# Attention and two MoE layers on one core: the product of pp and w_in as float32 products of one head each

## The chip, the cores and the metric

One core of one Trainium2 chip runs the whole program. The metric is device time in microseconds (us): the median of three runs of the kernel before is 1433.44 us (1433.17 to 1434.22).

## The reference, cut to what matters

```python
p_packed = sm_attn(p, k, v)              # 32 packed rows per head: softmax(p k^T / 8) v
out = sm_attn(q, p_packed, p_packed)     # batch 8, heads 8, 576 tokens, head size 64
x = out.transpose(0, 2, 1, 3).reshape(4608, 512)
h = x @ w_in                             # w_in is 512 x 2048
g = s * np.maximum(h, 0.0) ** 2 + b
x2 = g @ w_out                           # w_out is 2048 x 512
a, b2 = x2 @ w1, x2 @ w2                 # second layer, 1024 wide
return ((a * b2) @ w3) @ w_out2
```

The kernel does not form `x`. With A the softmax of the second attention (tokens by 8 heads x 32 packed rows, 256 wide) and pp the packed result of the first, x @ w_in is A @ W' with W' = pp @ w_in, where each head's 32 rows of pp meet the 64 rows of w_in that belong to that head. W' is 256 x 2048 for each batch. This case is about how W' is made.

## The kernel before, in words

**Stages.** From 0 to about 90 us the first attention of batches 0 to 3 runs (units u of four heads, N1 = 8 units), w_in is decoded from the 64-bit input, and W' of batches 0 and 1 is made (`W_pair`, L524). From 92 to about 840 us a loop over 256 steps (L1011) does the first MoE layer: a batch has 32 steps (two halves of 288 tokens, 16 blocks of 128 columns of d_ff). A step has six products into `hps` (A by W') and twelve into `xps` (g by w_out), each a `mm3`: three float32r products of high and low parts in place of one float32 product. Between those steps stand the rest: the second attention of later batches (`qtp` L186 transposes, `scp` L200, `atp` L234), the first attention of batches 4 to 7 (units 8 to 15, placed by `plan`, L911, into steps that have room: `ktp` L352, `s1p` L378, `etp` L444, `pvp` L466, `ppp` L480), the decoding of w1, w2, w3 and w_out2 (`job`), and W' of batches 2 to 7. After 840 us comes the second MoE layer, which this case does not touch.

**pp.** `ppT` holds pp transposed: 128 partitions are two heads of 64, and for each pair of heads and each batch 64 columns, the two heads' 32 packed rows side by side. Half of those 128 x 64 numbers are zeros, since a head's columns are zero in the other head's 64 partitions (L471 multiplies by `rec`, which has a zero for the other head). `D_ev` (L477) writes it from a transpose.

**W' of batches 0 and 1** (`W_pair`, eight calls in iterations 6 to 9 of the first loop): two tiles of w_in (two pairs of heads, 512 columns) and both batches, four float32 products of 128 rows by 64 columns, one to each half of two PSUM tiles. A float32 product is two matmul records in the trace. Evicted by ACT as the high part, DVE as the low part (batch 0), and ACT as a plain copy (batch 1), which is split later (`split_wp`).

**W' of batches 2 to 7** (three times 16 tiles of w_in, one per step from step 17 of an odd batch on, NW = 16): `W_load` (L860) brings a tile of the decoded w_in back from DRAM four steps ahead, `W_split` (L503) splits it on ACT and DVE one step ahead, and `W_tile` (L509) makes both batches' columns of one pair of heads in one `mm3` of 128 rows by 128 columns, N = 512, into one PSUM tile of the pair `a2`. `pp_split` (L489) splits pp first, once per pair of batches (steps 46, 110 and 172). The steps of `wsteps` (L906) have no room for `plan`.

**Order.** Each engine runs its instructions in the order that they were given when the program was built. A scheduler sets that order, from a timeline simulation of its own; only what `keep_in_program_order` names is tied down. PSUM tiles named `a2` are two buffers that everything beside `hps` and `xps` shares in the loop of 256 steps.

Of the kernel before, what the change touches and what calls it, by code (L numbers as in the profile page):

```python
# [22 lines left out]
def fused_kernel(  # L23
# [80 lines left out]
    ident = const.tile([P, P], F32, name="ident")  # L104
    odd = const.tile([P, 2, 1], F32, name="odd")
# [58 lines left out]
    if True:  # L164
# [322 lines left out]
        pps, sw, wst, wch = {}, {}, {}, {}  # L487

        def pp_split(bp):  # L489

            hi = stg.tile([P, NPAIR, P], F32R, tag="pph", name="pph", bufs=1)
            lo = stg.tile([P, NPAIR, P], F32R, tag="ppl", name="ppl", bufs=1)
            for o in range(2):
                for bb in range(2):
                    c = slice(64 * (bb ^ o), 64 * ((bb ^ o) + 1))
                    split(hi[:, o::2, c], lo[:, o::2, c], ppT[:, bp, o::2, bb, :], pin="hi")
            pps[bp] = (hi, lo)
# [5 lines left out]
        def W_split(k, src):  # L503
            hi = stg.tile([P, FC], F32R, tag="sh", name="sh", bufs=2)
            lo = stg.tile([P, FC], F32R, tag="sl", name="sl", bufs=2)
            split(hi, lo, src)
            sw[k] = (hi, lo)

        def W_tile(bp, k, ps):  # L509

            fc, pr = divmod(k, NPAIR)
            ph, pl = pps[bp]
            wh, wl = sw.pop(k)
            mm3(ps, ph[:, pr, :], pl[:, pr, :], wh, wl, True, True)
            if pr == 0:
# [3 lines left out]
            h0, h1 = (slice(64 * ((pr + bb) % 2), 64 * ((pr + bb) % 2 + 1)) for bb in range(2))  # L519
# [4 lines left out]
        def W_pair(j, ps):  # L524

            fc, c = divmod(j, 2)
            for pr in (2 * c, 2 * c + 1):
                for bb in range(2):
                    h = slice(64 * ((pr + bb) % 2), 64 * ((pr + bb) % 2 + 1))
                    ins = nc.tensor.matmul(  # L530
                        ps[bb][h], ppT[:, 0, pr, bb, :], win_at(fc * NPAIR + pr), start=True, stop=True
                    )
                    if bb:
                        tc.keep_in_program_order(ins)
            if c == 0:
                wch[0, fc] = wch_tiles()
                wst[1, fc] = wch_p.tile([P, 2, FC], F32, tag="wpst", name="wpst", bufs=4)
            hi, lo = wch[0, fc]
            split(hi[:, c], lo[:, c], ps[0])
            nc.scalar.copy(wst[1, fc][:, c], ps[1])  # L540
# [68 lines left out]
        make_identity(nc, ident)  # L609
        for h in range(4):  # L610
# [23 lines left out]
        def w_pair(j):  # L634
            wps = q_ps if j % 2 == 0 else kt_ps
            W_pair(j, [wps("wps") for _ in range(2)])
# [230 lines left out]
        WR = 17  # L867
# [37 lines left out]

        wsteps = {2 * FB1 * n_ + WR + w for n_ in range(1, B - 1, 2) for w in range(NW)}  # L906

# [67 lines left out]
        PPS = (46, 110, 172)  # L975
# [467 lines left out]
```

## Time and profile before

| | before |
|---|---|
| median of 3 runs | 1433.44 us |
| the profiled execution | 1435.98 us |
| its span, first to last instruction | 1434.2 us |
| granted TensorE clock, mean | 0.997 |
| busy: PE, DVE, ACT | 98%, 63%, 52% |

PE is the matmul engine (TensorE) and PEld its weight loads; DVE is VectorE and ACT is ScalarE. A record of PE has a duration that includes the way through the array, so records overlap. What a matmul costs the engine is the time from its start to the next one's start; the timeline view shows starts. Consecutive records of one kind are merged there into one row: its start, the time to the end of its last record, and how many.

### The profile page before, as it was taken

The page shows a single profiled execution, that of the slowest core. Times are in us where ns is not written, and L with a number is a line of the kernel's source. Part 1 is how long each engine was busy: PE and PEld are TensorE (multiplying, and loading weights), DVE is VectorE, ACT ScalarE, POOL GpSimd, SP SyncE. Part 2 cuts the span into 40 slices and gives each one's busy share as a digit, 9 for nine tenths or more (in the row PEclk, how much of TensorE's full clock was granted, in tenths as well). Part 3 has the DMA queues.
Part 4 walks back from the last instruction along what each step waited for, and adds up shares of the span by engine and source line. Part 5 has one row for each costly group of instructions (what it writes and reads, how often), then busy time and mean ns, then how long its engine had stood idle before and what let it go on. Part 6 is the DMA issues. An engine that isn't in the chain of part 4 may idle for free.

```text
span 1434.2 us, 28727 instructions
## 1 busy us (share of the span) xinstructions
PE 1410.8 (98%) x11233; PEld 1332.8 (93%) x11233; DVE 899.5 (63%) x1770; ACT 750.7 (52%) x1617; POOL 3.9 (0%) x38
## 2 busy tenths in 40 slices
PE   8999999999999999999999999999999999999997
PEld 6579999999999999998999988999999999999997
DVE  5786544656556666567878346476675756757556
ACT  4686555776566766557867534143332433324323
POOL 0000000000000000000000000000000000000000
PEclk9999999999999999999999999999999999999999
DMA  8975221232453543454655352775675857757551
GB/s 294 342 242 167 60 65 34 83 91 83 138 154 101 156 127 100 124 161 134 182 163 195 96 185 82 236 245 166 194 226 166 251 167 207 222 161 216 161 162 44
DMA packets 177574, 228.90 MB, mean 160 GB/s; under 512 B 55584, under 2 KB 109856, under 8 KB 177440
## 3 DMA queue, kind: packets, MB, share of 16 engines
q1 hardware_dynamic: 177440, 227.08, 52.4%
q8 instruction: 89, 1.46, 0.4%
q14 instruction: 45, 0.37, 0.1%
HBM read 182.98 MB, written 44.04 MB: 158 GB/s over the span
## 4 chain that ended last, share of the span: by engine, by line
PE 89%; DMA 3%; ACT 3%; DVE 3%; SPq 1%; issue 1%; ACTq 0%; DVEq 0%
PE xps L86 9%; PE xps L89 9%; PE xps L90 9%; PE prod L86 7%; PE prod L90 7%; PE prod L89 7%; PE hps L90 4%; PE hps L86 4%; PE hps L89 4%; PE yps L89 4%; PE yps L90 4%; PE yps L86 4%; PE scp L200 2%; DMA raw<-in_moe_w_in_dram 2%; PE qtp L186 1%; PE wps L530 1%
## 5 line engine op out<-in xcount | busy, mean ns | idle before, releaser
L89 PE MATMUL xps<-gl,wo 128*128 128x288 f32 (+1 forms) x1024 | 302.5, 298 | 1.2 <-DVE gl L757 1.2
L90 PE MATMUL xps<-gh,wo 128*128 128x288 f32 (+1 forms) x1024 | 301.3, 298 | 0.0
L86 PE MATMUL xps<-gh,wo 128*128 128x288 f32 (+1 forms) x1024 | 291.9, 299 | 0.8 <-ACT xst L783 0.8
L86 PE MATMUL prod<-xc,whl 128*128 128x384 f32 x672 | 226.2, 337 | 3.1 <-ACT Ta L1083 2.0
L90 PE MATMUL prod<-xc,whl 128*128 128x384 f32 x672 | 225.0, 335 | 0.0
L89 PE MATMUL prod<-xc,whl 128*128 128x384 f32 x672 | 224.8, 335 | 0.0
L89 PEld LDWEIGHTS xps<-gl,wo 128*128 128x128 f32 x1024 | 192.7, 188 | 4.9 <-issue 1.9
L90 PEld LDWEIGHTS xps<-gh,wo 128*128 128x128 f32 x1024 | 192.4, 188 | 2.8 <-issue 1.9
L86 PEld LDWEIGHTS xps<-gh,wo 128*128 128x128 f32 x1024 | 188.1, 188 | 3.8 <-ACT xst L783 1.0
L745 ACT ACTIVATE r<-hps 128x288 f32<-128x288 f32 x256 | 104.4, 409 | 118.9 <-PE hps L90 111.3
L757 DVE TENSOR_TENSOR gl<-r,gh 128x288 fp32r<-128x288 f32 x256 | 115.7, 454 | 80.6 <-ACT r L754 77.0
L1083 ACT COPY Ta<-prod 128x384 f32<-128x384 f32 x96 | 46.1, 480 | 215.4 <-PE prod L90 214.6
L86 PE MATMUL hps<-ATh,wpl 128*128 128x288 f32 x512 | 153.0, 299 | 1.4 <-ACT r L745 0.7
L90 PE MATMUL hps<-ATh,wph 128*128 128x288 f32 x512 | 152.7, 298 | 0.0
L89 PE MATMUL hps<-ATl,wph 128*128 128x288 f32 x512 | 152.4, 298 | 0.0
L89 PE MATMUL yps<-w4c,op 128*128 128x256 f32 x504 | 142.2, 282 | 0.0
L90 PE MATMUL yps<-w4c,op 128*128 128x256 f32 x504 | 142.1, 282 | 0.0
L86 PE MATMUL yps<-w4c,op 128*128 128x256 f32 x504 | 140.9, 280 | 0.0
L86 PEld LDWEIGHTS prod<-xc,whl 128*128 128x128 f32 x672 | 126.2, 188 | 7.6 <-ACT Ta L1083 4.1
L89 PEld LDWEIGHTS prod<-xc,whl 128*128 128x128 f32 x672 | 126.2, 188 | 0.0
L90 PEld LDWEIGHTS prod<-xc,whl 128*128 128x128 f32 x672 | 126.1, 188 | 0.0
L754 ACT ACTIVATE r<-r 128x288 f32<-128x288 f32 x256 | 112.8, 444 | 4.9
(167 smaller groups left out, 2519.5 us busy)
## 6 DMA issues: line engine op xcount, KB each, us to landing
whl<-whl SPq DMA_DIRECT2D x336, 256.0 KB, 3.1
raw<-in_moe_w_dram SPq DMA_DIRECT2D x32, 512.0 KB, 4.7
raw<-in_moe_w_out_dram SPq DMA_DIRECT2D x24, 512.0 KB, 5.1
x<-win SPq DMA_DIRECT2D x48, 256.0 KB, 2.8
q<-in_q_dram SPq DMA_DIRECT2D x72, 128.0 KB, 3.7
x<-xst SPq DMA_DIRECT2D x16, 576.0 KB, 3.8
out_dram<-O SPq DMA_DIRECT2D x72, 128.0 KB, 2.4
raw<-in_moe_w_in_dram SPq DMA_DIRECT2D x16, 512.0 KB, 7.1
```

Of the source, the lines that this page charges most:

```text
L86: ins = nc.tensor.matmul(ps, wl, xh, start=start, stop=False, **kw)
L89: nc.tensor.matmul(ps, wh, xl, start=False, stop=False, **kw)
L90: nc.tensor.matmul(ps, wh, xh, start=False, stop=stop, **kw)
L186: nc.tensor.transpose(ps[:, pr * P:pr * P + n], src[:n, 2 * pr:2 * pr + 2, :].rearrange("p h d -> p (h d)"), ident[:n, :n],)
L200: nc.tensor.matmul(ps[sl, c:c + 64], qT[b, t][:, pr, sl], ppT[:, b // 2, pr, b % 2, :], start=True, stop=True,)
L530: ins = nc.tensor.matmul(ps[bb][h], ppT[:, 0, pr, bb, :], win_at(fc * NPAIR + pr), start=True, stop=True)
L745: nc.scalar.activation(r, ps[:, :HS], AF.Relu)
L754: nc.scalar.activation(r, r, AF.Square)
L757: nc.vector.tensor_tensor(out=gl[:, :HS], in0=r, in1=gh[:, :HS].bitcast(F32), op=ALU.subtract)
L1083: tc.keep_in_program_order(nc.scalar.copy(out, src))
```

## The change

The array has, for products of 64 rows by 32 columns, eight places: two halves of the rows by four quarters of the columns. The change makes W' of all batches by `W_pair`, now with products of one head each: 64 rows of `ppT` by the 32 columns of one head, float32, N = 512. Two tiles of w_in (i), two batches (bb) and the two heads of a pair (r) make eight products, and the places are chosen so that the eight differ in place. That puts the two heads of the odd batch the other way round, so `ppT` of odd batches is written with its two groups of 32 columns exchanged: `D_ev` multiplies by a permutation `swap` in place of the transpose by `ident`. In the loop of 256 steps the 48 tiles of w_in become 24 pairs, at the steps WAT of odd batches, loaded at the steps WLD; `W_split`, `pp_split` and `W_tile` are gone, and a pair takes both `a2` buffers at once. The tags of some later tiles change with that (`wl` in place of `sh`, `sl`, `pph`).

```diff
@@ D_ev
-            nc.tensor.transpose(ps[:, :P], PVX.pop(u).rearrange("p o d -> p (o d)"), ident)
+            src = PVX.pop(u).rearrange("p o d -> p (o d)")
+            if b % 2:
+                nc.tensor.matmul(ps[:, :P], src, swap, start=True, stop=True)
+            else:
+                nc.tensor.transpose(ps[:, :P], src, ident)
...
-        def W_tile(bp, k, ps):
...
-            mm3(ps, ph[:, pr, :], pl[:, pr, :], wh, wl, True, True)
...
-            split(hi[h0, pr // 2], lo[h0, pr // 2], ps[h0])
-            d = wst[2 * bp + 1, fc][h1, pr // 2, :]
-            nc.scalar.copy(d, ps[h1])
...
+        def W_pair(bp, j, ps, src):
+
+            fc, c = divmod(j, 2)
+            for i in range(2):
+                for bb in range(2):
+                    for r in range(2):
+                        rows = slice(D * r, D * (r + 1))
+                        o = NP * (r ^ bb)
+                        h = 64 * (i ^ bb) + o
+                        ins = nc.tensor.matmul(
+                            ps[bb][h:h + NP], ppT[rows, bp, 2 * c + i, bb, o:o + NP], src[i][rows],
+                            start=True, stop=True,
+                        )
+                        if bp == 0 and bb:
+                            tc.keep_in_program_order(ins)
...
             split(hi[:, c], lo[:, c], ps[0])
-            nc.scalar.copy(wst[1, fc][:, c], ps[1])
+            nc.scalar.copy(wst[2 * bp + 1, fc][:, c], ps[1])
...
+        for o in range(2):
+            nc.gpsimd.tensor_copy(
+                swap.rearrange("p (a o n) -> p a o n", o=2, n=NP)[:, :, o],
+                ident.rearrange("p (a o n) -> p a o n", o=2, n=NP)[:, :, 1 - o],
+            )
...
-        def W_load(k):
-            wx[k] = dec.tile([P, FC], F32, tag="x", name="x", bufs=XB)
-            nc.sync.dma_start(out=wx[k], in_=win_d[k])
+        def W_load(j):
+            wx[j] = []
+            for k in (2 * j, 2 * j + 1):
+                wx[j].append(stg.tile([P, FC], F32, tag="wl", name="wl", bufs=6))
+                nc.sync.dma_start(out=wx[j][-1], in_=win_d[k])
...
-        WR = 17
+        WAT = (19, 20, 24, 25, 27, 28, 30, 31)
+        WLD = (13, 14, 16, 20, 21, 25, 26, 28)
...
-        wsteps = {2 * FB1 * n_ + WR + w for n_ in range(1, B - 1, 2) for w in range(NW)}
+        wsteps = {2 * FB1 * n_ + w for n_ in range(1, B - 1, 2) for w in WAT}
...
+            nn, k = divmod(idx, 2 * FB1)
+            if nn % 2 == 1 and nn + 1 < B:
+                for j in range(len(WAT)):
+                    if k == WLD[j]:
+                        W_load(j)
+                    if k == WAT[j]:
+                        W_pair((nn + 1) // 2, j, [a2_ps("wps") for _ in range(2)], wx.pop(j))
```

**The order on PE in the loop of 256 steps.** Before, around the first W' tiles of batches 2 and 3 (out<-in by the names of the program, then the size of the output; L86, L89 and L90 are the three products of a `mm3`):

```order
L89 MATMUL xps<-gl,wo_1932 128x288
L90 MATMUL xps<-gh,wo_1932 128x288
L86 MATMUL xps<-gh,wo_1932 128x288
L86 MATMUL wps<-sh,ppl 128x512
L89 MATMUL wps<-sl,pph 128x512
L90 MATMUL wps<-sh,pph 128x512
L89 MATMUL xps<-gl,wo_1932 128x288
L90 MATMUL xps<-gh,wo_1932 128x288
L86 MATMUL wps<-sh,ppl 128x512
L89 MATMUL wps<-sl,pph 128x512
L90 MATMUL wps<-sh,pph 128x512
L86 MATMUL hps<-ATh,wpl 128x288
```

And in the changed program, around the first two pairs of the same batches (L507 is the product of `W_pair` there):

```order
L90 MATMUL hps<-ATh,wph 128x288
L86 MATMUL xps<-gh,wo_1617 128x288
L89 MATMUL xps<-gl,wo_1617 128x288
L90 MATMUL xps<-gh,wo_1617 128x288
L507 MATMUL wps<-wl,ppT 32x512 x4
L86 MATMUL xps<-gh,wo_1617 128x288
L89 MATMUL xps<-gl,wo_1617 128x288
L90 MATMUL xps<-gh,wo_1617 128x288
L86 MATMUL xps<-gh,wo_1617 128x288
L89 MATMUL xps<-gl,wo_1617 128x288
L90 MATMUL xps<-gh,wo_1617 128x288
L507 MATMUL wps<-wl,ppT 32x512 x4
```

The three products of a tile stood together, 48 times. The eight of a pair stand as two runs of four, the first run into one PSUM tile (batch bb = 0) and the second into the other, with full-array products between them. Over the loop there are 44 such runs: 40 of four and 4 of eight. Four of the runs follow `scp` directly.

**The order on PE in the first stage.** Before, from the fifth pair on (winx is decoded w_in; `etp` and `wps` are 128 rows by 64 columns, `pvp` and `s1p` 64 by 32, `ppp` the full array):

```order
L460 MATMUL pvp<-v,E1T 32x64 x32
L530 MATMUL wps<-winx_150,ppT 64x512 x2
L430 MATMUL etp<-ident,E_1011 64x64 x10
L530 MATMUL wps<-winx_150,ppT 64x512 x2
L480 MATMUL ppp<-ident,pvx 128x128
L430 MATMUL etp<-ident,E_1011 64x64 x8
L530 MATMUL wps<-winx_151,ppT 64x512 x2
```

And in the changed program, where L461 is the line of `pvp` and L431 that of `etp`:

```order
L461 MATMUL pvp<-v,E1T 32x64 x36
L507 MATMUL wps<-winx_151,ppT 32x512 x4
L431 MATMUL etp<-ident,E_1022 64x64 x10
L507 MATMUL wps<-winx_151,ppT 32x512 x4
L485 MATMUL ppp<-ident,pvx 128x128
L431 MATMUL etp<-ident,E_1022 64x64 x8
L507 MATMUL wps<-winx_152,ppT 32x512 x4
```

Where two products stood, four of half the rows and half the columns stand. Over the first stage the 32 products before make 15 runs, one of four and the rest of two; the 64 after make 17 runs: three of eight, six of four, and eight of one to three.

## Rows read from the trace of the kernel before

**Rows 1.** The page: busy us of each engine, share, instructions; then the chain by engine.

```profile
PE 1410.8 (98%) x11233; PEld 1332.8 (93%) x11233; DVE 899.5 (63%) x1770; ACT 750.7 (52%) x1617; POOL 3.9 (0%) x38
...
PE 89%; DMA 3%; ACT 3%; DVE 3%; SPq 1%; issue 1%; ACTq 0%; DVEq 0%
```

**Rows 2.** Two stretches: length, busy us of PE, PEld, DVE, ACT, POOL, clock, DMA.

```profile
54.50:90.00 35.50, 34.57 (x571) 17.48 (x570) 28.04 (x66) 24.99 (x56) 0.57 (x8) 1.00 0.94 330
...
95.00:840.00 745.00, 740.82 (x6172) 707.68 (x6171) 460.98 (x1122) 495.51 (x1165) 2.68 (x24) 1.00 0.40 120
```

**Rows 3.** Timeline of PE, a W' tile in the loop: start us, us, instruction, count.

```profile
249.56 0.30 PE L90 MATMUL xps<-gh,wo 128*128 128x288 f32 x1
249.70 0.39 PE L86 MATMUL wps<-sh,ppl 128*128 128x512 f32 x1
...
250.40 0.29 PE L86 MATMUL xps<-gh,wo 128*128 128x288 f32 x1
```

**Rows 4.** Groups by form, 95 to 840 us: count, busy us, mean ns, idle before.

```profile
L81 DVE TENSOR_TENSOR wpl<-wps,wph 64x512 fp32r<-64x512 f32 x48 | 33.1, 689 | 24.1 <-ACT wph L78 23.0
...
L81 DVE TENSOR_TENSOR sl<-x,sh 128x512 fp32r<-128x512 f32 x48 | 32.8, 682 | 13.0 <-ACT sh L78 12.5
...
L78 ACT CAST sh<-x 128x512 fp32r<-128x512 f32 x48 | 29.7, 619 | 13.7 <-DMA x<-win 13.2
...
L78 ACT CAST wph<-wps 64x512 fp32r<-64x512 f32 x48 | 27.8, 580 | 16.4 <-PE wps L90 15.8
...
L522 ACT COPY wpst<-wps 64x512 f32<-64x512 f32 x48 | 27.8, 578 | 1.8 <-DVE wpl L81 1.0
...
L86 PE MATMUL wps<-sh,ppl 128*128 128x512 f32 x48 | 19.3, 403 | 0.8 <-ACT wpst L522 0.5 <-ACT qT L192 0.4
```

**Rows 5.** Timeline of PE around a late s1p: float32, 64 rows by 32 columns.

```profile
176.61 0.29 PE L86 MATMUL xps<-gh,wo 128*128 128x288 f32 x1
176.74 0.30 PE L89 MATMUL xps<-gl,wo 128*128 128x288 f32 x1
176.97 0.69 PE L378 MATMUL s1p<-kT,pTd 64*32 64x288 f32 x8
177.59 0.40 PE L90 MATMUL xps<-gh,wo 128*128 128x288 f32 x1
177.83 0.29 PE L86 MATMUL xps<-gh,wo 128*128 128x288 f32 x1
```

**Rows 6.** Timeline of PE in the first stage: W' pairs beside etp, s1p and pvp.

```profile
61.27 1.08 PE L530 MATMUL wps<-winx,ppT 128*64 128x512 f32 x4
62.27 0.62 PE L370 MATMUL s1p<-kT,pTd 64*32 64x256 f32 x2
...
81.83 0.97 PE L460 MATMUL pvp<-v,E1T 64*32 64x64 f32 x50
82.73 1.08 PE L530 MATMUL wps<-winx,ppT 128*64 128x512 f32 x4
83.64 0.75 PE L430 MATMUL etp<-ident,E 128*64 128x64 f32 x20
84.22 1.03 PE L530 MATMUL wps<-winx,ppT 128*64 128x512 f32 x4
85.18 0.33 PE L480 MATMUL ppp<-ident,pvx 128*128 128x128 f32 x1
```

**Rows 7.** The page's DMA issues: out<-in, count, KB each, median us to landing.

```profile
x<-win SPq DMA_DIRECT2D x48, 256.0 KB, 2.8
```

**Rows 8.** Timeline: the last ppp of the first stage, with its releaser.

```profile
89.76 0.33 PE L480 MATMUL ppp<-ident,pvx 128*128 128x128 f32 x1 [0.41 <-DVE pvx L471]
```

**Rows 9.** Timeline of PE around a late ppp, a transpose on the full array.

```profile
605.26 0.27 PE L480 MATMUL ppp<-ident,pvx 128*128 128x128 f32 x1
605.37 0.60 PE L186 MATMUL qtp<-ident,q 128*128 128x128 f32 x4
```

More of the change, by code (lines that the diff above doesn't have):

```diff
@@ L104, in fused_kernel @@
     ident = const.tile([P, P], F32, name="ident")
+    swap = const.tile([P, P], F32, name="swap")
     odd = const.tile([P, 2, 1], F32, name="odd")
@@ L484, in D_ev @@
             )
[L487 to L497, printed above, removed]
+        wst, wch = {}, {}
         def wch_tiles():
@@ L501, in wch_tiles @@
                     wch_p.tile([P, 2, FC], F32R, tag="wpl", name="wpl", bufs=4))
[L503 to L507, printed above, removed]
-        def W_tile(bp, k, ps):
-            fc, pr = divmod(k, NPAIR)
-            ph, pl = pps[bp]
-            wh, wl = sw.pop(k)
-            mm3(ps, ph[:, pr, :], pl[:, pr, :], wh, wl, True, True)
-            if pr == 0:
+        def W_pair(bp, j, ps, src):
[12 more added lines that the diff above has]
+                            tc.keep_in_program_order(ins)
+            if c == 0:
                 wch[2 * bp, fc] = wch_tiles()
@@ L518, in W_tile @@
             hi, lo = wch[2 * bp, fc]
-            h0, h1 = (slice(64 * ((pr + bb) % 2), 64 * ((pr + bb) % 2 + 1)) for bb in range(2))
-            split(hi[h0, pr // 2], lo[h0, pr // 2], ps[h0])
-            d = wst[2 * bp + 1, fc][h1, pr // 2, :]
-            nc.scalar.copy(d, ps[h1])
[L524 to L538, printed above, removed]
             split(hi[:, c], lo[:, c], ps[0])
-            nc.scalar.copy(wst[1, fc][:, c], ps[1])
+            nc.scalar.copy(wst[2 * bp + 1, fc][:, c], ps[1])
         def split_wp(b, fc):
@@ L635, in w_pair @@
             wps = q_ps if j % 2 == 0 else kt_ps
-            W_pair(j, [wps("wps") for _ in range(2)])
+            W_pair(0, j, [wps("wps") for _ in range(2)], [win_at(2 * j + i) for i in range(2)])
         for i in range(N1 + OFF):
@@ L904, in at @@
             late.setdefault(step, []).append(fn)
-        wsteps = {2 * FB1 * n_ + WR + w for n_ in range(1, B - 1, 2) for w in range(NW)}
+        wsteps = {2 * FB1 * n_ + w for n_ in range(1, B - 1, 2) for w in WAT}
+        assert not wsteps & a2use
         def room(step):
@@ L974, in fused_kernel @@
         end3 = plan(range(N1 + 4, NU), max(end2 + 5, 98))
-        PPS = (46, 110, 172)
-        assert end2 <= PPS[1] and end3 <= PPS[2], (end2, end3)
+        LATE = 172
+        assert end2 <= 2 * FB1 * 3 + WAT[0] and end3 <= LATE, (end2, end3)
         def load_wo2(c):
@@ L992, in split_wo2 @@
             else:
-                wo2[c] = tuple(stg.tile([P, DM], F32R, tag=t, name="wo2", bufs=2) for t in ("sh", "sl"))
+                wo2[c] = tuple(stg.tile([P, DM], F32R, tag="wl", name="wo2", bufs=6) for _ in range(2))
             split(*wo2[c], wo2st.pop(c))
@@ L1016, in fused_kernel @@
                 wo_load(idx + AHEAD + 4)
-            if idx in PPS:
-                pp_split(PPS.index(idx) + 1)
-            if idx == PPS[2]:
+            if idx == LATE:
                 ctxl.close()
@@ L1022, in fused_kernel @@
                 p3["S"] = ctxl.enter_context(pool("ss"))
-            for d in (4, 1, 0):
-                nn, k = divmod(idx + d - WR, 2 * FB1)
-                if nn > 0 and nn % 2 == 1 and nn + 1 < B and k < NW:
-                    if d == 4:
-                        W_load(k)
-                    elif d == 1:
-                        W_split(k, wx.pop(k))
-                    else:
-                        W_tile((nn + 1) // 2, k, a2_ps("wps"))
+            nn, k = divmod(idx, 2 * FB1)
[5 more added lines that the diff above has]
+                        W_pair((nn + 1) // 2, j, [a2_ps("wps") for _ in range(2)], wx.pop(j))
             nn, k = divmod(idx - 20, 2 * FB1)
@@ L1156, in V_mm @@
                 w4c[i] = bp_.tile([P, 2, 7, NH], F32R, name=f"w4c_{i}")
-                p3["b12"] = stg.tile([P, NH], F32, tag="pph", name="b12", bufs=1)
+                p3["b12"] = stg.tile([P, NH], F32, tag="wl", name="b12", bufs=6)
                 p3["T"] = wch_p.tile([P, 4, NH], F32, tag="wpl", name="w4s", bufs=4)
```

## The prediction
> **What bounds the kernel now.** I read the page first: PE is busy for 98% of the span and makes 89% of the chain that ended last; DVE and ACT stand at 63% and 52% [rows 1]. Then the busy time by stretches, cut where W' is made: in the first attention (54.5 to 90 us) PE is busy 34.57 of 35.50 us, in the loop of 256 steps (95 to 840 us) 740.82 of 745.00, at a granted clock of 1.00 in both [rows 2]. So in both places the change is worth what it does to PE's own time, and what ACT or DVE are spared is worth at most the 4.2 us that PE sat idle in the loop. The third view is the timeline, since a busy time overlaps: there I take the distance between starts.
>
> **W' in the loop, before.** One tile runs from 249.70 to 250.40 us, 0.70 us for three float32r products on the full array, and the product before it keeps its ordinary distance (249.56 to 249.70) [rows 3]: nothing is paid for entering. There are 48 tiles [rows 4]: 48 x 0.70 = **33.6 us** of PE.
>
> **W' in the loop, now.** What a run of 64-by-32 products costs is shown by the late `s1p`: eight records, that is four float32 products in four places, N = 288 [rows 5]. The ordinary distance is 0.13 us (176.61 to 176.74). The `s1p` starts 0.23 us after the product before it, so going over to small places costs 0.10; its run lasts 0.62 us (176.97 to 177.59); and the first full-array product after it takes 0.24 us to the next, so going back costs 0.11. For N = 512 I have the run from the old pairs of the first stage, two places at a time and two records in each: 1.00 us between neighbours of another form (61.27 to 62.27) and 0.91 or 0.96 where a neighbour has the same form [rows 6]. Scaling agrees: 0.62 us holds two rounds of 288 columns, 1.00 us two rounds of 512, which is 0.85 ns for each added column and round. So one run costs 0.10 + 1.00 + 0.11, about **1.20 us, whether four places are filled or eight**: a round lasts as long as one product, and filling more places only adds to the work done in it.
>
> The step that decides is therefore how many runs there are. The diff speaks of eight places at a time, which would be 24 runs. The built order has 44 in the loop: the first four products of a pair write one PSUM tile, the other four the second, and full-array products were placed between. 44 x 1.20 = 52.8 us. Four runs stand right behind `scp`, which has to leave and enter anyway, and save about 0.2 us each: 52.0 us. Against 33.6 us that is **+18.4 us**.
>
> **What that spares.** For each of the 48 tiles ACT loses the split's cast (0.62 us) and DVE its subtraction (0.68 us); and the evictions (0.58 and 0.58 us on ACT, 0.69 us on DVE) come once for two tiles [rows 4]: ACT 29.7 + half of 55.6, or 57 us less, DVE 32.8 + half of 33.1, or 49 us less; `pp_split` goes as well. All of it lies beside PE. What can come back is idle time of PE: 4.2 us in the loop [rows 2], of which the tile's own first product waited 0.8 us [rows 4]. Against it stands a new wait: a pair holds both `a2` buffers until ACT and DVE have emptied them, and whoever wants `a2` next on PE (the next pair, `scp`, `qtp`, `atp`, a unit of the late attention) is queued ahead of the `xps` and `hps` products that follow it. The scheduler placed the runs for that. I take -2 us for the two together, between -4.2 (all idle time gone) and +2 (no relief, some 0.05 us at each run).
>
> **The loads** are the same 48 transfers of w_in, now two at once and into six buffers of their own, three to eight steps ahead (WLD against WAT) where they were four. A step of 18 products at 0.13 us lasts at least 2.3 us, so the shortest lead is 7 us; a load landed 2.8 us after its issue [rows 7]. If SP's queue held one up, PE would stand at that run; the three buffers `x`, shared with the decoding, get freer. Zero. `plan` places the late units by other steps; their work is the same. Zero.
>
> **The first stage.** Before: 32 products, two at a time, so 16 times two rounds, each time 0.91 to 1.00 us [rows 6], 16 x 0.96 = 15.4 us. Now 64 products in 17 runs, of which two (a 3 and a 4 beside `s1p`) can go together: again about 16 times two rounds. The halving that the eight places could give is spent on splitting. What changes is the neighbours: next to `etp` a form change is new (0.1 us each way), next to `pvp` and `s1p` one is gone, and where places differ, `pvp` or `s1p` can run beside a W' run. I take -1.5 us, between -3.5 (four runs wholly hidden beside `pvp` or `s1p`, 0.9 us each) and +2 (twenty new form changes). A shorter chain at the end helps little: the last `ppp` waited for DVE (0.41 us) [rows 8].
>
> **`swap`.** A transpose on the full array takes 0.11 us to the next start (605.26 to 605.37) and is one record [rows 9]; an ordinary float32 product is two. Eight of the sixteen `ppp` change: 8 x 0.11 = +0.9 us. The two copies on POOL are made once at the start, behind `ident`, and first needed in the third unit. Zero.
>
> **The sum.** +18.4 - 2 - 1.5 + 0.9 = +15.8 us on the profiled execution's 1435.98, so 1451.8 us. The median of the runs lies 2.5 us lower (1433.44), and with the same difference it becomes **1449 us**. Low end of the terms: 18.4 - 4.2 - 3.5 + 0.5 = +11; high end: 18.4 + 2 + 2 + 0.9 = +23; that is 1444 to 1457.
>
> **A page's rule against the change.** A run of four now writes one PSUM tile from both halves of the rows. `pvp` does the same before: its four heads take the four quarters of the columns with the halves of the rows in turn, into one tile. 50 of its records of 64 columns take 0.90 us (81.83 to 82.73), 18 ns each; at 0.85 ns a column one alone lasts 54 ns, so more than two at a time were under way [rows 6]. The Trainium skill (TensorEngine Tiling (Array Packing), Gotcha 1: PSUM Pressure) says that different row tiles cannot access the same PSUM bank simultaneously. By that rule each run would need its rounds twice. This trace speaks against it.
>
> **The rivals.**
> - *Row halves exclude each other in one tile.* Each of the 44 + 16 runs has its two rounds doubled, + 0.86 us each, +51 us: 1500 us. 18 ns per `pvp` record speaks against it; that `pvp` is short and the new products are eight times as long is all that speaks for it. Chance 0.03.
> - *The pair of buffers becomes the wait.* An eviction is a cast of 0.58 us on ACT, then 0.69 us on DVE, and for the other buffer a copy of 0.58 us [rows 4]. If PE stands for half a microsecond at each of the 44 runs, that is +22 us more: 1471 us. It decides once the next user of `a2` stands less than about 1.3 us (ten full-array products) behind a run. Runs three or six products apart are there, but for the other buffer. Chance 0.10.
> - *The eight places are filled after all, and it gets faster.* Four products of `s1p` run together in 0.62 us, so places work side by side [rows 5]. If PE held a first half back, or took the second forward, and filled the places of a pair in one round in spite of the order, the loop has 24 runs of 1.20 us (28.8, or -4.8 us) and the first stage half its rounds (-7.7 us): with `swap` -11.6 us, 1422 us. The point from which it decides is 33.6 / 1.20 = 28 runs in the loop. Against it: the products between the two halves take the whole array. Chance 0.04.
> - *More relief than I count.* All idle time gone, the first stage at its best and cheaper switches, so that some 11 of the 15.8 us are missing: about 1437 us, which is within the resolution or just slower. Chance 0.06.
> - The forecast: 0.77.
>
> **How the numbers follow.** A measurement of this kernel tells apart about 0.2%, 2.9 us. Faster: the third rival and a little of the fourth, 0.05. Within 0.2%: part of the fourth, 0.04. Slower: the forecast, the first two and the rest, 0.91. The range takes the ends of the terms, 1444 to 1457, and reaches down into the fourth rival and up into the milder waits of the second: 1440 to 1459.
>
> **What would show it.** Right: in the loop, 40-odd `wps` runs, most of eight records (four products), whose start lies 1.0 us before the next row, entered after 0.23 us and left at 0.24 us; the stretch of the loop 14 to 20 us longer and the first stage within 3 us of before; ACT and DVE busy times some 57 and 49 us lower, with PE as full as before. Wrong: a run of eight records that takes 1.8 us (the rule), idle time of PE ended by ACT or DVE before `wps` or `scp` beyond 5 us (the buffers), or fewer than 30 runs.

## The result, and the profile after

| | before | after |
|---|---|---|
| median | 1433.46 us (1433.17 to 1434.22, 4 runs) | 1449.80 us (1446.50 to 1452.95, 4 runs) |
| ratio, 95% interval | | 1.0113 (1.0089 to 1.0136) |
| the same again, later (`e0_again`) | 1433.91 us (17 runs) | 1447.03 us (1446.90 to 1448.04, 4 runs) |
| ratio, 95% interval | | 1.0097 (1.0084 to 1.0110) |
| profiled executions, two of each | 1435.98 and 1432.92 us | 1446.50 and 1448.04 us |

The change makes the kernel slower by about 1%, 13 to 16 us, where +15.8 us was forecast.

The page of after, busy time of each engine and the chain by engine, answers to [rows 1]:

```profile
PE 1424.6 (99%) x11545; PEld 1314.6 (91%) x11545; DVE 851.2 (59%) x1686; ACT 701.1 (49%) x1509; POOL 4.2 (0%) x40
...
PE 94%; DMA 2%; DVE 2%; ACT 1%; issue 0%; SPq 0%; ACTq 0%
```

and the two stretches (length, busy us of PE, PEld, DVE, ACT, POOL, clock, DMA) to [rows 2]:

```profile
54.50:90.00 35.50, 33.26 (x684) 17.08 (x682) 28.48 (x71) 25.72 (x59) 0.38 (x8) 1.00 1.03 365
95.00:840.00 745.00, 744.71 (x6338) 679.12 (x6338) 410.18 (x1031) 441.68 (x1050) 2.73 (x24) 1.00 0.39 118
```

DVE and ACT are 51 and 54 us less busy in the loop (49 and 57 were forecast), and PE is now busy for all of it. PE was the bound before and is more so now: what the two other engines were spared could buy no more than the 4 us that PE had stood idle.

A run of four products in the loop, from PE's timeline (start us, time to the end of the last record, instruction, records):

```profile
255.26 0.29 PE L89 MATMUL xps<-gl,wo 128*128 128x288 f32 x1
255.40 0.29 PE L90 MATMUL xps<-gh,wo 128*128 128x288 f32 x1
255.62 1.06 PE L507 MATMUL wps<-wl,ppT 64*32 64x512 f32 x8
256.61 0.40 PE L86 MATMUL xps<-gh,wo 128*128 128x288 f32 x1
256.85 0.29 PE L89 MATMUL xps<-gl,wo 128*128 128x288 f32 x1
```

The run starts 0.22 us after the product before it (ordinary: 0.14), its neighbour starts 0.99 us after it, and the next one 0.24 us later: 0.09 + 0.99 + 0.11 beyond the ordinary distances, 1.19 us, where 0.10 + 1.00 + 0.11 had been put together from `s1p` and the first stage. The order has 44 runs, 40 of them like this one.

The groups by form in the same stretch (count, busy us, mean ns, idle before) show the work that went:

```profile
L507 PE MATMUL wps<-wl,ppT 64*32 64x512 f32 x384 | 46.9, 601 | 0.0
...
L81 DVE TENSOR_TENSOR wpl<-wps,wph 128x512 fp32r<-128x512 f32 x24 | 16.5, 689 | 21.9 <-ACT wph L78 21.9
...
L78 ACT CAST wph<-wps 128x512 fp32r<-128x512 f32 x24 | 14.0, 585 | 18.7 <-PE wps L507 18.4
L518 ACT COPY wpst<-wps 128x512 f32<-128x512 f32 x24 | 14.0, 584 | 15.8 <-PE wps L507 15.8
```

The split (`sh`, `sl`) is gone and each eviction comes 24 times at the duration it had 48 times in [rows 4]: filling 128 partitions costs ACT and DVE no more than filling 64.

**Where the time went.** The way through the program is cut at the first W' record, the first `xps` and the last `xps`. Within the loop, W' is the time between starts at a run and its neighbours beyond the ordinary distance. Idle PE is the gap in its records ahead of an instruction that waited, and between two `xps` or `hps` products the whole delay of the start; by the gaps alone it is 4.17 and 3.40 us before. Two profiled executions of each kernel, in us; the differences are first against first and second against second:

| stretch | before | after | difference |
|---|---|---|---|
| start to the first W' | 54.55, 54.99 | 55.88, 56.06 | +1.1 to +1.3 |
| first W' to first `xps` | 40.05, 39.50 | 39.85, 40.84 | -0.2 to +1.3 |
| loop, first to last `xps` | 743.34, 741.80 | 753.65, 754.63 | +10.3 to +12.8 |
| of it W' | 34.88, 34.90 | 52.05, 52.15 | +17.2 |
| of it idle PE | 4.82, 3.73 | 0.29, 0.96 | -2.8 to -4.5 |
| of it everything else | 703.64, 703.17 | 701.31, 701.52 | -1.7 to -2.3 |
| after the loop | 596.26, 594.86 | 595.35, 594.69 | -0.2 to -0.9 |

W' behaves as forecast, but the loop gets back over twice as much elsewhere as was granted it, and ahead of the loop there is a loss where a gain was forecast. Most of its first row is not the products' doing: both profiles of after were granted half the clock for 6.8 us ahead of the first W', both of before for 3.4, and with 3.4 us or none the same first stage takes 55.0 to 55.2 us to that point (`e2_first_only`, `e7_gate_first`, `e9_dve_new_first`). The experiments go after W', the idle time and the first stage.

### The profile page after: what moved, and what is told of

Read it like the earlier page. It is cut to its first block, busy times and chain, and to the rows that moved or that the text cites. A ratio compares the mean times of both kernels' runs of the same rounds, so it can differ in the third digit from the quotient of the medians.

```text
span 1444.7 us, 29157 instructions
## 1 busy us (share of the span) xinstructions
PE 1424.6 (99%) x11545; PEld 1314.6 (91%) x11545; DVE 851.2 (59%) x1686; ACT 701.1 (49%) x1509; POOL 4.2 (0%) x40
## 4 chain that ended last, share of the span: by engine, by line
PE 94%; DMA 2%; DVE 2%; ACT 1%; issue 0%; SPq 0%; ACTq 0%
PE xps L89 10%; PE xps L90 10%; PE xps L86 10%; PE prod L86 8%; PE prod L90 7%; PE prod L89 7%; PE hps L86 5%; PE hps L90 5%; PE hps L89 5%; PE yps L89 4%; PE yps L90 4%; PE yps L86 4%; PE wps L507 3%; PE scp L201 2%; PE qtp L187 1%; PE w4a L86 1%
## 5 line engine op out<-in xcount | busy, mean ns | idle before, releaser
L89 PE MATMUL xps<-gl,wo 128*128 128x288 f32 (+1 forms) x1024 | 305.4, 299 | 0.0
L90 PE MATMUL xps<-gh,wo 128*128 128x288 f32 (+1 forms) x1024 | 304.8, 299 | 0.0
L86 PE MATMUL xps<-gh,wo 128*128 128x288 f32 (+1 forms) x1024 | 302.3, 299 | 0.0
L86 PE MATMUL prod<-xc,whl 128*128 128x384 f32 x672 | 226.3, 337 | 2.8 <-ACT Ta L1066 1.8
L90 PE MATMUL prod<-xc,whl 128*128 128x384 f32 x672 | 225.0, 335 | 0.0
L89 PE MATMUL prod<-xc,whl 128*128 128x384 f32 x672 | 224.9, 335 | 0.0
L86 PEld LDWEIGHTS xps<-gh,wo 128*128 128x128 f32 x1024 | 191.7, 188 | 10.4 <-issue 9.3
L90 PEld LDWEIGHTS xps<-gh,wo 128*128 128x128 f32 x1024 | 192.5, 188 | 9.4 <-issue 8.9
L89 PEld LDWEIGHTS xps<-gl,wo 128*128 128x128 f32 x1024 | 192.7, 188 | 8.3 <-issue 7.3
L86 PE MATMUL hps<-ATh,wpl 128*128 128x288 f32 x512 | 154.5, 302 | 0.0
L89 PE MATMUL hps<-ATl,wph 128*128 128x288 f32 x512 | 152.8, 298 | 0.0
L90 PE MATMUL hps<-ATh,wph 128*128 128x288 f32 x512 | 152.3, 298 | 0.0
L90 PE MATMUL yps<-w4c,op 128*128 128x256 f32 x504 | 142.2, 282 | 0.0
L89 PE MATMUL yps<-w4c,op 128*128 128x256 f32 x504 | 142.1, 282 | 0.0
L86 PE MATMUL yps<-w4c,op 128*128 128x256 f32 x504 | 140.9, 280 | 0.0
L86 PEld LDWEIGHTS prod<-xc,whl 128*128 128x128 f32 x672 | 126.2, 188 | 7.3 <-ACT Ta L1066 3.8
L89 PEld LDWEIGHTS prod<-xc,whl 128*128 128x128 f32 x672 | 126.2, 188 | 0.0
L90 PEld LDWEIGHTS prod<-xc,whl 128*128 128x128 f32 x672 | 126.1, 188 | 0.0
```

Source lines behind the costliest of these rows:

```text
L86: ins = nc.tensor.matmul(ps, wl, xh, start=start, stop=False, **kw)
L89: nc.tensor.matmul(ps, wh, xl, start=False, stop=False, **kw)
L90: nc.tensor.matmul(ps, wh, xh, start=False, stop=stop, **kw)
```

## The experiments

Twelve runs follow, two of them repeats of the two kernels, in three jobs; each job has its own runs of the kernel before (1433.91 us, 17 runs; 1433.69 us, 15 runs; 1433.30 us, 9 runs). Line numbers in the rows are those of each kernel.

### The runs, or the products: `e0_again`, `e1_gate`, `e11_second_first`, `e10_one_gate`

`e0_again` is the changed kernel unchanged; its result stands in the first table. Its loop takes 754.63 us, within what the theory of the runs gave, with 0.96 us of idle PE in it.

> The changed kernel once more, for its spread (1446.5 to 1453.0 us in four runs, where the kernel before stays within 1.1 us). Theory of the runs (each entry into the small places costs a run of 1.2 us, 44 of them in the loop): the loop is 753 to 755 us from the first xps to the last again, so what varies lies outside it, at a lower granted clock. Theory of the buffers (PE waits for the pair of a2 buffers, more in some executions): the loop itself is longer in a slower execution, with idle time of PE over 3 us in it.

`e1_gate` makes one run of eight out of two of four. Ahead of a pair, PE makes two small products that write the pair's two buffers, so it stands until both are free, and then the eight are kept in order:

```diff
+            if bp:
+                for bb in range(2):
+                    gw = wo_t[0][:, 0, :]
+                    nc.tensor.matmul(ps[bb][:, :32], gw[:, :P], gw[:, :32], start=True, stop=True)
...
-                        if bp == 0 and bb:
+                        if bp or bb:
                             tc.keep_in_program_order(ins)
```

> The changed kernel, but in the loop each pair's eight products are pinned in one run, behind two short full-array products (32 columns, overwritten afterwards) that take the two a2 buffers. Theory of the runs: 24 runs of about 1.22 us and 48 gates of some 0.06 us in place of 44 runs, 52 us become 32 us, so the loop is about 20 us shorter (734 us) and the time about 1430 us. Theory of the buffers: both buffers are now held from the first gate on, so waits grow; the time stays at 1448 us or above.

Measured: **1428.56 us** (1426.21 to 1429.41, 6 runs), ratio 0.9963 (0.9951 to 0.9975), faster than both kernels. A gate and a run of eight, from PE's timeline:

```profile
252.96 0.30 PE L86 MATMUL xps<-gh,wo 128*128 128x288 f32 x1
253.09 0.18 PE L504 MATMUL wps<-wo 128*128 128x32 f32 x1
253.20 1.09 PE L511 MATMUL wps<-wl,ppT 64*32 64x512 f32 x16
254.22 0.40 PE L89 MATMUL xps<-gl,wo 128*128 128x288 f32 x1
254.45 0.29 PE L90 MATMUL xps<-gh,wo 128*128 128x288 f32 x1
```

Sixteen records take 1.02 us to the next start, eight took 0.99: twice the work for 0.03 us. The gate right ahead of the run costs little as well: 0.13 + 0.11 us from the product before it to the run, where a run without a gate is entered after 0.22. The same 192 products cost PE 33.4 us in 24 runs with their gates, and 52.1 us in 44.

`e11_second_first` is `e3_loop_only` (below: the loop of the change, the first stage of before) with the order within a pair turned, which gives 39 runs, 9 of them of eight:

```diff
-            for i in range(2 if bp else 0):
-                for bb in range(2):
-                    for r in range(2):
+            for bb, i, r in [(bb, i, r) for bb in (1, 0) for i in range(2) for r in range(2)] if bp else ():
...
-                        if bp == 0 and bb:
+                if (bb, i, r) != (1, 0, 0):
```

> e3_loop_only (44 runs in the loop, 1444.84 us, 52.05 us of PE for W') with the order within a pair turned: the four products of the second buffer first, all eight kept in order. The scheduler then makes 39 runs, 9 of them of eight. Theory of the runs (1.18 us each, full or not): 46.0 us of PE for W', so 5 x 1.18 = 5.9 us less: 1439 us (1437.5 to 1440.5). Rival (the time goes with the products or with the records, 192 and 384 in both): 1444.8.

Measured: **1439.74 us** (1438.91 to 1440.50, 5 runs), 5.1 us below `e3_loop_only` for five runs fewer; its loop is 748.08 us against 753.23. With the products and records the same, the time goes with the number of runs, 1.0 us each. W' alone fell by 8.0 us (52.05 to 44.03), more than five runs are worth, and the `s1p` rose by 2.2 against `e3_loop_only`. Two of the W' runs here are mixed with an `s1p`, four records at a time, and the two kinds take 1.47 us together (297.99 to 299.46 for one), part of which counts as `s1p`; and two `s1p` that stand joined in `e3_loop_only` have come apart.

`e10_one_gate` stands at the end of the line of improvements, with one gate for each pair (it builds on `e8_dve_evict`, below):

```diff
-                for bb in range(2):
-                    gw = wo_t[0][:, 0, :]
-                    nc.tensor.matmul(ps[bb][:, :32], gw[:, :P], gw[:, :32], start=True, stop=True)
+                gw = wo_t[0][:, 0, :]
+                nc.tensor.matmul(ps[1][:, :32], gw[:, :P], gw[:, :32], start=True, stop=True)
```

> e8_dve_evict with one gate for each pair, on the buffer that comes second, in place of two. Runs in the loop: 24, as before. W' took PE 33.8 us in e4 with 24 runs and 48 gates; 24 x 1.18 is 28.4, so a gate costs about 0.1 us and this one 24 x 0.1 = 2.4 us less: 1422.6 us if e8 comes to 1425 (1421.5 to 1424.5). Rival (the gate's cost is that of going over to small places, which is paid anyway): within 0.8 us of e8_dve_evict.

Measured: **1425.59 us** (1424.65 to 1426.69, 5 runs), ratio 0.9942 (0.9930 to 0.9954), the fastest version here: 0.95 us below `e8_dve_evict`, where 2.4 was expected, and just above the rival's bound of 0.8. The loop shortens by 1.03 us (734.76 to 733.73), but 0.75 of that is idle time that `e8_dve_evict` had and this run has not; 0.3 us is left for the 24 gates. The rows say why: in `e8_dve_evict` one gate of each pair stands right ahead of the run, where it costs 0.02 us (product, gate and run start at 252.45, 252.58 and 252.69), and the other stands alone among full-array products, where it costs 0.11. All 24 that are left here stand alone. So the rival has the mechanism right: a gate at the run's door costs next to nothing, since going over to small places is paid anyway.

### The idle time of the loop: `e5_ballast`, `e6_before_again`

What PE waited for in the loop of before (us, times, longest) was spread over many things:

```profile
PE xps L89 <- DVE gl L757: 1.2, 2, 0.8
PE xps L86 <- ACT xst L783: 0.8, 1, 0.8
PE hps L86 <- ACT r L745: 0.7, 2, 0.4
PE hps L86 <- DVE wpl L81: 0.7, 1, 0.7
PE wps L86 <- ACT wpst L522: 0.5, 1, 0.5
PE wps L86 <- ACT qT L192: 0.4, 1, 0.4
```

In after one row is left (in `e0_again` another one, of 1.0 us, ended by ACT):

```profile
PE atp L235 <- DVE wpl L81: 0.3, 1, 0.3
```

`e5_ballast` is `e3_loop_only` with the split put back as work that nobody reads:

```diff
+            for t in src if bp else ():
+                sh_ = ap.tile([P, FC], F32R, tag="sh", name="sh", bufs=1)
+                split(sh_, sh_, t)
```

> e3_loop_only (44 runs, old first stage, 1444.84 us, no idle time of PE in the loop) with the split of each of the 48 w_in tiles put back on ACT and DVE, its results read by nobody: a cast of 0.62 us and a subtraction of 0.68 us for each tile. Theory (the 4.8 us that PE lost in the loop of before came from ACT and DVE being late with their other work, and the change gave them back by taking that work away): idle time of PE in the loop comes back, 2 to 5 us, so 1447 to 1450. Rival (the idle time belonged to the tile's own chain, split, three products and two evictions each): under 1 us, 1444 to 1446.

Measured: 1445.61 us (1445.08 to 1447.13, 4 runs), 0.8 us above `e3_loop_only`; PE idle in the loop 1.14 us. Of its waits, the three longest:

```profile
PE ktp L353 <- ACT E L407: 0.4, 1, 0.4
PE xps L89 <- DVE gl L753: 0.3, 1, 0.3
PE xps L86 <- ACT xst L779: 0.2, 1, 0.2
```

The load of the split alone brings back at most a quarter to a third of the idle time, and the changed kernel without it shows 0.29 and 0.96 us, so my theory falls as it was put. That the rest belonged to the tile's own chain, as the rival has it, is not shown: of the waits of before, only the 0.7 for `wpl` and the 0.5 for `wpst` name that chain, and the largest name `gl`, `xst` and `r`, other work of DVE and ACT. The ballast puts 29 us of work back on ACT and 32 on DVE, of the 54 and 51 by which they were less busy; the doubled evictions stay away, and the built order is another with the ballast in it. Which part weighed most stays open.

> The kernel before once more, for a second profile: if the terms taken from its first profile are a property of the kernel, PE's idle time between the first and the last xps is again 4 to 5.5 us, that stretch 742.5 to 744.5 us, and the way from the first W' to the first xps 39.5 to 40.5 us. If they are one execution's luck, the idle time differs by more than 2 us.

Measured: one execution of 1432.92 us, PE idle 3.73 us, loop 741.80 us, first W' to first `xps` 39.50 us. Idle time and loop lie somewhat below what was given, within the 2 us that would have made them luck. The idle time is a property of the kernel (six of its seven longest waits lie within 2 us of places that waited in the first profile), but one execution tells it only to about 1 us, and the loop to 1.5.

### The first stage: `e2_first_only`, `e3_loop_only`, `e7_gate_first`, `e9_dve_new_first`

`e2_first_only` is before with the new products in the first stage alone; `e3_loop_only` is after with the old ones there:

```diff
+            if bp == 0:
+                for pr in (2 * c, 2 * c + 1):
+                    for bb in range(2):
+                        h = slice(64 * ((pr + bb) % 2), 64 * ((pr + bb) % 2 + 1))
+                        ins = nc.tensor.matmul(
+                            ps[bb][h], ppT[:, 0, pr, bb, :], src[pr % 2], start=True, stop=True
+                        )
+                        if bb:
+                            tc.keep_in_program_order(ins)
-            for i in range(2):
+            for i in range(2 if bp else 0):
...
-            if b % 2:
+            if b % 2 and b > 1:
```

> The kernel before with the new products in the first stage alone (batches 0 and 1; swap for batch 1); the loop has the old split and the 48 tiles. Theory of the runs: 16 or 17 runs as against 16 before, so 1432 to 1435 us. Rival (the first stage carries the loss, or the spread): 1437 us or more, with a spread of over 3 us.

Measured: 1436.27 us (1434.63 to 1442.62, 12 runs), ratio 1.0024 (1.0014 to 1.0034): +2.4 us, a loss where between -2 and +1 was expected, short of the rival's 1437.

> The changed kernel with the old 128-by-64 products in the first stage; the loop as in the change (44 runs). Theory of the runs: the loop 753 us, the time 1446 to 1451 us. Rival (the first stage carries a part of the loss): 1443 us or less.

Measured: 1444.84 us (1444.10 to 1445.71, 4 runs), ratio 1.0080 (1.0067 to 1.0093), 2.2 us below `e0_again` and between the two ranges that were given. So the change is +10.9 us in the loop and +2.2 to +2.4 ahead of it, and the two add up to the 13.1 us of `e0_again`.

`e9_dve_new_first` asks the same once more in an improved kernel: it is `e8_dve_evict` (below) with the first stage of the change, that is `e1_gate` with the one line that `e8_dve_evict` changes.

> e8_dve_evict with the first stage as the change has it (64-by-32 products, swap for the first pair of batches). Theory (the first stage loses 2 to 2.5 us, as without the gates): 1427.3 us, 2 to 3 us above e8_dve_evict. Rival (it is worth nothing either way, and the 2.2 us between e0_again and e3_loop_only were where the half clock fell): within 0.8 us of e8_dve_evict.

Measured: 1428.39 us (1427.17 to 1430.92, 5 runs), 1.85 us above `e8_dve_evict`, just under the 2 to 3 of the theory and above the rival's 0.8; the ranges of the two overlap, so the two pairs before this one carry the reading. Its profiled execution shows full clock from 6 to 1419 us, and that of `e8_dve_evict` in this stretch, so here no clock hides or makes the difference: first W' to first `xps` takes 40.94 us with the new products and 39.63 with the old. What PE's starts give for that stretch, in us, old against new: W' 15.40 and 13.95, `s1p` 2.79 and 1.54, `pvp` 6.26 and 5.60, `etp` 4.85 and 5.73, `ppp` 1.44 and 1.54, idle 0.41 and 4.09. The products save 2.4 us, and 3.7 us of waiting take their place. The waits of PE in that stage, for `e9_dve_new_first`,

```profile
PE ppp L483 <- DVE wpl L81: 1.6, 1, 1.6
PE ppp L483 <- DVE pvx L472: 1.6, 1, 1.6
PE wps L511 <- DVE ATl L81: 0.9, 1, 0.9
```

and for `e8_dve_evict`:

```profile
PE ppp L483 <- DVE pvx L472: 0.4, 1, 0.4
```

The changed kernel has the same three in both its profiles (0.5 to 1.5, 0.9 and 1.6 us). Two can be read. DVE's timeline (start us, duration) ahead of the W' run at 77.73, in `e9_dve_new_first`:

```profile
76.06 0.68 DVE L81 TENSOR_TENSOR wo<-x,wo 128x512 fp32r<-128x512 f32 x1
76.66 0.69 DVE L159 SCALAR_TENSOR_TENSOR x<-raw,x 128x512 uint32<-128x512 uint32 x1
77.26 0.42 DVE L81 TENSOR_TENSOR ATl<-atp,ATh 128x256 fp32r<-128x256 f32 x1
```

W' wants the PSUM buffer that `atp` holds until `ATl` ends at 77.68, and `ATl` stands in DVE's queue behind two steps of the decoding of w_out. The last unit, ACT first and then DVE:

```profile
86.83 0.59 ACT L522 COPY wpst<-wps 128x512 f32<-128x512 f32 x1 [0.74 <-PE wps L511]
87.32 0.43 ACT L437 COPY E1T<-etp 128x320 f32<-128x320 f32 x1
87.64 0.70 ACT L144 ACTIVATE x<-raw 128x512 f32<-128x512 f32 x1
88.37 0.43 DVE L147 TENSOR_SCALAR x<-x 128x512 int32<-128x512 int32 x1 [2.81 <-ACT x L144]
88.83 0.69 DVE L152 SCALAR_TENSOR_TENSOR x<-raw,x 128x512 int32<-128x512 int32 x1
89.44 0.68 DVE L81 TENSOR_TENSOR wpl<-wps,wph 128x512 fp32r<-128x512 f32 x1
90.04 0.68 DVE L159 SCALAR_TENSOR_TENSOR x<-raw,x 128x512 uint32<-128x512 uint32 x1
90.64 0.28 DVE L472 TENSOR_TENSOR pvx<-pvp,rec 128x128 f32<-128x128 f32 x1
```

`pvp` was done at 89.51, but `pvx` had to wait for a low part and a decoding step, and PE stood until 91.07. In before the same `pvx` waited 0.06 us, because PE came later.

DVE ends the stage, but it is not short of time: it had stood 2.81 us for ACT's decoding step (87.64), and that one stands in ACT's queue behind the copy of a W' buffer (86.83), which waited for PE. In `e8_dve_evict`, where PE makes that pair's second half in one piece, the copy starts at 85.12, the decoding step at 86.41 and `pvx` at 89.39, 1.25 us earlier, which is nearly the whole of the 1.31 us between the two stretches. In the new order a `ppp` stands between the first product of that half (84.33) and the other three (85.72), and the one takes as long as the three. So PE's savings turn into waits at the end of a chain PE, ACT, DVE, PE. This is read from the rows; an order without the split was not run. In `e2_first_only` the last steps come in another order, with a wait of 1.7 us at the same place.

The first of the three waits stands before the second product with `swap`, and the row names a DVE instruction that had ended 0.4 us earlier; `e1_gate`, with the same first stage, does not have it, and what released it stays open.

`e7_gate_first` is `e1_gate` with gates in the first stage too, and the eight kept in order there:

```diff
-            if bp:
-                for bb in range(2):
-                    gw = wo_t[0][:, 0, :]
+            for bb in range(2):
+                gw = wo_t[0][:, 0, :] if bp else ident
```

> e1_gate (1428.56 us) with gates in the first stage too: two small products on the two PSUM tiles, then the eight products of a pair together, 8 runs of eight in place of 17 mixed ones. PE's time for W' there falls from 13.95 us to about 8 x 1.2 plus gates, 11.5. Theory (the first stage ends with DVE's chain to the last pvx, so PE's savings come back as idle time): within 1 us of e1_gate, 1427.6 to 1429.6, and PE's idle time there rises from 2.5 to about 5 us. Rival (PE bounds the stage and the waits were those of split pairs): 1426, idle time not above 2.5 us.

Measured: 1433.59 us (1428.33 to 1435.92, 11 runs), ratio 0.9996 (0.9985 to 1.0007), 5 us above `e1_gate`: outside what either theory gave. Stretches of the profiled execution (1435.62 us):

```profile
74.80:77.30 2.50, 0.85 (x18) 0.48 (x18) 1.85 (x5) 1.04 (x2) 0.00 (x0) 0.99 1.01 390
77.30:90.90 13.60, 13.60 (x165) 7.85 (x151) 7.22 (x16) 6.20 (x16) 0.00 (x0) 0.50 1.02 382
90.90:97.80 6.90, 4.84 (x124) 3.82 (x123) 4.65 (x10) 4.81 (x11) 0.00 (x0) 0.99 0.39 127
97.80:101.20 3.40, 3.40 (x14) 3.11 (x13) 3.33 (x6) 1.79 (x5) 0.00 (x0) 0.50 0.57 182
```

PE stood 1.68 us at a gate (74.8 to 76.5, for the same `ATl`), and from 77.3 us the chip granted half the clock for 13.6 us, and again at 97.8. Of its executions the one with a mean clock of 0.991 that is not the profiled one took 1435.33 us, and those at 0.997 1431.32 and 1428.33: with the clock nearly full the gates still gain nothing over `e1_gate`, which fits a stage that does not end with PE's own work, and with it halved they lose.

### Who holds the pair: `e4_gate_old_first`, `e8_dve_evict`

`e4_gate_old_first` is `e3_loop_only` with the gates and the order of `e1_gate` in the loop.

> The two parts that did best, put together: in the loop the gated pairs (24 runs of eight products, as in e1_gate, 1428.56 us), in the first stage the old 128-by-64 products. Theory (the new products of the first stage save PE 2.7 us and get it back as waits for DVE and ACT, so that stage loses 2 to 2.5 us on the whole, as e0_again against e3_loop_only and e2_first_only against before showed): 1426.3 us, between 1425 and 1427.5. Rival (what the first stage loses is only where the half clock fell in the first 24 us): 1428.5, as e1_gate.

Measured: 1428.23 us (1427.27 to 1430.91, 5 runs), no better than `e1_gate`, as the rival had it. But its profile shows that its loop is another: PE's timeline and two stretches around 488 us,

```profile
485.78 0.38 PE L86 MATMUL xps<-gh,wo 128*128 128x288 f32 x1
487.84 0.28 PE L513 MATMUL wps<-wo 128*128 128x32 f32 x1 [1.69 <-ACT wpst L531]
488.06 1.30 PE L520 MATMUL wps<-wl,ppT 64*32 64x512 f32 x16
```

```profile
485.00:488.80 3.80, 2.12 (x26) 1.31 (x25) 0.00 (x0) 2.08 (x5) 0.00 (x0) 1.00 0.61 237
488.80:492.20 3.40, 3.40 (x20) 2.91 (x13) 1.83 (x4) 1.95 (x5) 0.00 (x0) 0.50 0.49 154
```

and ACT's timeline there:

```profile
482.63 0.59 ACT L78 CAST wph<-wps 128x512 fp32r<-128x512 f32 x1 [3.49 <-PE wps L520]
486.65 0.66 ACT L144 ACTIVATE x<-raw 128x512 f32<-128x512 f32 x1 [3.43 <-DMA w<-x]
487.22 0.57 ACT L531 COPY wpst<-wps 128x512 f32<-128x512 f32 x1
```

The copy that empties the pair's second buffer stands in ACT's queue behind a decoding step that waits 3.43 us for a transfer. The gate waits for that copy, and the 3.4 us at half the clock that follow cost PE about 1.7 us more, since they hold the work of 1.7. `e1_gate` has the same wait there (2.11 us) at full clock. `e8_dve_evict` gives the copy to DVE:

```diff
-            nc.scalar.copy(wst[2 * bp + 1, fc][:, c], ps[1])
+            (nc.vector.tensor_copy if bp else nc.scalar.copy)(wst[2 * bp + 1, fc][:, c], ps[1])
```

> e4_gate_old_first (1428.23 us) with the second buffer of a pair emptied by DVE in the loop, not by ACT. In e4 and e1 a gate stood 1.7 and 2.1 us at 486 us: ACT's queue had a cast of the w_out decoding, waiting for a transfer, ahead of that copy, while DVE was idle; in e4 half the clock followed for 3.4 us, which cost 1.7 us more. Theory (that queue is what holds the pair): the wait is gone, PE's idle time in the loop under 0.7 us, the clock full through the loop, 1425 us (1424 to 1426.5). Rival (the pair waits for its loads or for DVE): a wait of over 1 us stays at this place, and the time within 1 us of 1428.2.

Measured: **1426.54 us** (1425.66 to 1428.74, 5 runs), 1.7 us below `e4_gate_old_first`; PE idle 0.75 us in the loop, its clock full there, and the waits that are left are elsewhere:

```profile
PE atp L235 <- DVE wpl L81: 0.5, 1, 0.5
PE scp L201 <- ACT qT L193: 0.3, 1, 0.3
```

The theory's place and cause are right; the time lies at the upper end of what it gave. What it is worth is less sure: with the new first stage the same line changed nothing on the median (`e1_gate` 1428.56, `e9_dve_new_first` 1428.39), though the loop of the profiled execution shortened by 2.5 us. With this out of the way the old first stage is again the better one (`e9_dve_new_first`), which fits a tie of `e4_gate_old_first` and `e1_gate` that this wait and its clock made; one profile of each is all that shows it.

## Why the prediction was right, and where its steps were off

- **The price of a run: right.** 1.20 us forecast, 1.19 in the rows of after, and 52.1 us for 44 runs against 52.0. Runs of four and of eight take 0.99 and 1.02 us. The number of runs, read from the built order, decides: 44, 39 and 24 runs gave 1444.84, 1439.74 and 1425.59 us with the same first stage (the last one with the copy on DVE as well).
- **What it replaces: 1.2 us too low.** 48 x 0.70 = 33.6 us; the same accounting as for after gives 34.9. One tile had been read, and others stand beside products of another form. So +17.2, not +18.4 us.
- **What it spares: too small, and for half of it not foreseen.** -2 was taken, -2.8 to -4.5 us of idle time came back, and 1.7 to 2.3 us more in everything else. No W' run of after stands beside an `s1p`, `pvp` or `ktp`; what fell is those themselves, since the built order joins them more. Two pairs of `s1p` stand together, sixteen records in 0.65 us (300.83 to 301.48 for one) where eight take 0.62, and the `s1p` need 8.7 us in 14 runs for 9.9 in 16; `ktp` has 28 runs for 31 and `pvp` 8 for 9, each with one way in and out less. It is again a price by runs, and luck of the order as far as the prediction goes. The milder end of the buffers' wait did not come in the loop.
- **The first stage: the step that failed.** It had -1.5 us and +0.4 to +0.5 of `swap`; the pairs of runs show +2.2, +2.4 and +1.85. What the products cost PE was seen in kind, at half its size (-1.1 with `swap` was taken, 2.4 us were saved: less at W', `s1p` and `pvp`, more at `etp`, as named). Wrong was to take the saving off the path: "A shorter chain at the end helps little" was written of the last `ppp` alone, and [rows 8] already had PE waiting there. The stage ends with a chain over ACT and DVE, and the built order put two more waits in it, 3.7 us in place of the 2.4 saved. The wait for `ATl` is the second rival's mechanism, a buffer waiting for its eviction, in another place than it was looked for; the wait for `pvx` is not, it is a queue.
- **The sum: right in part by luck, as two errors of opposite sign make up for each other.** The loop was forecast at about +16.8 us (with its part of `swap`) and gave +10.9, and its stretch grew by 10.3 to 12.8 us where 14 to 20 was the sign of being right; the first stage was forecast at -1 and gave +2.2 to +2.4. Medians: +13.1 and +16.3 us against +15.8; the 3 us between the two fit the lower granted clock of the first four executions (last section). The fourth rival, more relief than counted, came in the loop for about half of what it asked: 5.9 of some 11 us.
- **The page's rule: does not hold here.** The Trainium skill (TensorEngine Tiling (Array Packing), Gotcha 1: PSUM Pressure) has different row tiles unable to access one PSUM bank at the same time. A run of four writes one PSUM tile from both row halves, each product its own 32 partitions, and the product behind it starts 0.99 us after it: two rounds, where that rule would need four. The rival's 1500 us fall.
- **The third rival fell:** PE did not fill the places in spite of the order. The loop's part of its sum is borne out where the order itself is changed: the eight places work at once, and at 24 runs the kernel is faster than before. An estimate by the slope of 1.0 us for each run, from 1439.74 us at 39 runs: the loop breaks even with 1433.3 us near 33 runs, above the 28 worked out from W' alone, since the relief counts too.

## What to carry to other kernels

The price of packing small products into the array is paid for each uninterrupted run, not for each product: read from the built order how many runs there are, and whether PE's queue holds the products together, before counting places. A gate, one cheap product that waits for the last resource, turned 44 runs into 24 and a loss of 11 us into a gain of 5 to 8 (the upper end with a copy on another engine and one gate fewer). And a saving on the engine that is 98% busy is still worth nothing in a stage that ends with another engine: ask at each stage which wait ends last there, what stands in that engine's queue ahead of the instruction that ends it, and what held that one up in turn.

## What was not expected of the hardware

- **Standing still can cost twice.** After a wait of 1.69 us in the middle of the loop PE was granted half its clock (0.50, that is 1.2 of 2.4 GHz) for 3.4 us (`e4_gate_old_first`), and after waits of 1.68 and 2.06 us in `e7_gate_first` for 13.6 and 3.4 us. After one of 2.11 us in `e1_gate` the clock stayed full, as it did after nine others of 1.5 to 1.7 us: of thirteen waits of 1.5 us or more behind the first 24 us of the profiles, three were followed by half the clock. A gate that waits can be dearer than its wait; what decides it, these runs do not show.
- **The clock and the spread.** The four executions of after, 1446.50, 1449.07, 1450.53 and 1452.95 us, had mean granted clocks of 0.996, 0.996, 0.994 and 0.993. Going from 0.996 to 0.993 is 0.6% of the time more at half clock, some 8.7 us of it, and worth about 4.4 of the 6.5 us between the ends (the means have three digits, so this is good to 1 or 2 us). Beside these, half the clock falls in the profiles into the last 3 to 6 us of every execution, and into the first 24 us of all but one, for 3.4 or 6.8 us at another place in nearly every one.
- **A small product costs by its place in the order.** A gate alone among full-array products costs 0.11 us (in `e10_one_gate` two products with a gate between them take 0.37 us from 256.89 to 257.26, and without one 0.26); right ahead of a run in small places it costs 0.02 (0.24 us from the product before it to the run in `e1_gate`, 0.22 without a gate).
